# Queries of the first 128 tokens taken block by block through the weight, and the third input tile's load held behind GpSimd's constants

## The chip, the cores and the metric

The kernel runs on one core of one Trainium2 chip. The metric is device time in microseconds (us) for one execution of the whole program. Before the change the median of three runs is 266.89 us (266.51, 266.89 and 267.87).

## What is computed

One transformer block with two parallel branches on 2048 tokens of width 640. Both branches read the same layer-normed input, and the result is their sum with the residual:

```python
x = A_x
xn = _layernorm(x, axis=-1)
return x + _A_ref(xn, A_wqkv, A_wo) + _B_ref(xn, B_w_gate, B_w_up, B_w_down)
```

Branch A is attention in 32 heads of width 20. Each token looks at 8 earlier tokens, itself included, two positions apart. `q`, `k` and `v` come from one product with `wqkv` (640 x 1920), and the result goes through `wo` (640 x 640). Branch B is a gated layer without a non-linearity: `(xn @ w_gate) * (xn @ w_up)`, width 1536, then `w_down`. All tensors are bf16.

## The kernel before, in words

The 2048 tokens are 16 tiles of 128, and four tiles make a chunk of 512 (`c`, with `ttl` the tile in it). The width of 640 is five blocks of 128 (`KT` = 5). A weight such as `wq` lies in SBUF as five row blocks `wq[:, i, :]`, one for each block `i` of the contraction; its columns are five output blocks `j`.

For each tile, `norm` (L383) takes the statistics on VectorE (L390, L397, L403: `bn_stats` of two halves, then `bn_aggr` into `mv`), the reciprocal root on GpSimd (L410, `rstd`), and the normalisation on VectorE (L419, `xn_t`). The tiles of chunk 0 are turned by TensorE (L458, `pst`), and ScalarE copies the result to `xnT` (L480); for tile 0, VectorE copies blocks 3 and 4. Later chunks are turned by DMA (L440).

Then come the products: `qk_group` (L504) for q and k, each output block `j` a group of five matmuls over `i` (L514, `psqk`), evicted by ScalarE to `qkT` (L531); `v_tile` (L548) for v (L558, `psv`); `gu` (L589) for the gate and the up product (L600, `psg`, `psu`); the logits (L660 on VectorE, `pw`; L676 on TensorE, `lps`); the weighted sum over v on VectorE (L786 to L800); and the last product with the residual (L849, L856, L879). v has another order of columns, so GpSimd permutes its weight first, one row block at a time: five copies `wv[:, i, :]` from `wo` (L308). Matmul `i` of the first v group waits for copy `i`.

The loads at the start are on three queues. ScalarE's queue issues `wq` in three transfers, of row blocks 0-1, 2-3 and 4 (L284). SyncE (SP) issues x tiles 0 to 3 (L261), `wk` and the v weight, which lies in the buffer `wo` for now (L269), x tile 4, the zeroed halo (L297), then x tiles 5 onward as their buffers come free (there are five). GpSimd's queue issues `wg` and `wu` (L326) after the four `rstd` of chunk 0. Ahead of all that GpSimd writes constants: the identity, the masks and others (L172 to L195), the last of them `mb` (L192).

The order of the work on each engine isn't written out by hand. Each piece of work is a step with an engine, an assumed cost, the steps it waits for, the pool buffers that it takes and a priority. `Plan.run` (L76) plays the steps on a model of the engines and emits them in the order that comes out. What an engine then does on the chip is fixed: it takes its instructions in that order and waits at each for the semaphores that it needs. A transfer from SP or ScalarE also waits until the transfer eight places earlier in the plan's order has landed, since eight semaphores go round.

TensorE's order in the head is: ten matmuls on zeros (L371), the turn of tile 0, three more on zeros, q of tile 0 in the groups `[0, 1]`, `[2]`, `[3, 4]` with the turn of tile 1 after the first of them, q of tile 1, turn of tile 2, k of tile 0, turn of tile 3, q of tile 2, and the other q and k products; then two gate and two up groups, and v. For tile 0 this is set by:

```python
groups = ([0, 1], [2], [3, 4], [5, 6, 7], [8, 9])
```

so the first ten matmuls run over all five row blocks of `wq` for output blocks 0 and 1.

Of the kernel before, what the change touches and what calls it, by code (L numbers as in the profile page):

```python
# [9 lines left out]
ACT = mybir.ActivationFunctionType  # L10
# [20 lines left out]
class Plan:  # L31
# [9 lines left out]
    def token(self, pool):  # L41
        return Token(pool)

    def add(self, eng, cost, fn, deps=(), prio=0.0, lag=0.0, takes=(), reads=(),
            nbytes=0, tight=False):
        s = Step(eng, cost, fn, deps, prio, lag, list(takes), list(reads), nbytes,
                 tight)
        for t in s.reads:
            t.left += 1
        self.steps.setdefault(eng, []).append(s)  # L50
        return s
# [65 lines left out]
def kernel(  # L117
# [11 lines left out]
    nc = tc.nc  # L129
    P = nc.NUM_PARTITIONS  # L130
# [8 lines left out]
    HALO = DIL * (W - 1)  # L139
    scale = float(Dh) ** -0.5  # L140
    EPS = 1e-5
    KT = D // P
# [7 lines left out]
    bf16, f32 = dt.bfloat16, dt.float32  # L150
# [8 lines left out]
    psum = ctx.enter_context(  # L159
        tc.tile_pool(name="psum", bufs=NPS, space=bass.MemoryType.PSUM)  # L160
    )
# [8 lines left out]
    with tc.manual_schedule():  # L170
# [32 lines left out]
        wq = const.tile([P, KT, D], bf16, name="wq")  # L203
# [20 lines left out]
        G = {}  # L224
        add, token = plan.add, plan.token

        def tl(name, shape, dtype, bufs):
            return work.tile(shape, dtype, name=name, tag=name, bufs=bufs)


        mm512, mm320, mm256, mm128 = 0.216, 0.136, 0.11, 0.057

        def act(n):
            return 0.06 + n / 1200.0
# [11 lines left out]
        def dma(fn, nbytes, deps=(), prio=None, takes=(), reads=(), q="SP", n=1, lag=0.0):  # L246
            if prio is None:
                spn[0] += 1
                prio = -5000.0 + spn[0]
            return add(q, n * issue[q], lambda: fn(queues[q]), deps=deps, prio=prio,  # L250
                       lag=lag, takes=takes, reads=reads, nbytes=nbytes)
# [4 lines left out]
        def load_x(t, ahead=0):  # L256
            T_x[t] = token("x")

            def fn(q):
                G["x", t] = tl("x_t", [P, D], bf16, 5)  # L260
                q.dma_start(  # L261
                    out=G["x", t][:], in_=x_flat[t * P : (t + 1) * P, :]
                )

            S_x[t] = dma(fn, P * D * 2 + ahead, takes=[T_x[t]])
# [13 lines left out]


        S_wq = []
        for lo, hi in ((0, 2), (2, 4), (4, KT)):
            def ld(lo=lo, hi=hi):
                nc.scalar.dma_start(  # L284
                    out=wq[:, lo:hi, :],
                    in_=A_wqkv[lo * P : hi * P, 0:D].rearrange("(i p) f -> p i f", p=P),
                )

            S_wq.append(add("ACT", 0.45, ld, prio=-5000.0 + lo, lag=4.45))
# [91 lines left out]
        S_xnT, T_xnT, S_tr, S_rs, S_xn = {}, {}, {}, {}, {}  # L381
# [115 lines left out]
        S_qk, T_qk, S_v, S_vst = {}, {}, {}, {}  # L497

        def qk_tile(c):
            if ("qk", c) not in G:  # L500
                G["qk", c] = tl("qkT", [P, 2 * KT, HALO + CS], bf16, 2)
            return G["qk", c]

        def qk_group(c, js, cols, prio):  # L504
            n = cols.stop - cols.start
            T = token("ps")

            def mm():
                ps = psum.tile([P, 512], f32, name="psqk", tag="ps")
                for a, j in enumerate(js):  # L510
                    w = wq if j < KT else wk
                    jj = j % KT
                    for i in range(KT):
                        nc.tensor.matmul(  # L514
                            ps[:, a * n : (a + 1) * n],
                            lhsT=w[:, i, jj * P : (jj + 1) * P],
                            rhs=G["xnT", c][:, i, cols],
                            start=(i == 0), stop=(i == KT - 1),
                        )
                G["psqk", c, js[0], cols.start] = ps  # L520

            tts = range(cols.start // P, cols.stop // P)
            deps = [d for q in tts for d in S_xnT[c, q]]
            deps += S_wq if min(js) < KT else []
            deps += [S_wk] if max(js) >= KT else []
            m = add("PE", len(js) * KT * (0.003 + n / 2400.0), mm, deps, prio, lag=0.15,
                    takes=[T], reads=[T_xnT[c]], tight=c == 0)

            def ev():
                ps = G["psqk", c, js[0], cols.start]  # L530
                nc.scalar.copy(  # L531
                    qk_tile(c)[:, js[0] : js[-1] + 1,
                               HALO + cols.start : HALO + cols.stop],
                    ps[:, 0 : len(js) * n].rearrange("p (j s) -> p j s", j=len(js)),
                )

            takes = []
            deps = [m]
            if c not in T_qk:
                T_qk[c] = token("qk")  # L540
                takes = [T_qk[c]]
                S_qk[c] = []
            else:
                deps.append(S_qk[c][0])
            S_qk[c].append(add("ACT", act(len(js) * n), ev, deps, prio, lag=0.1,
                               takes=takes, reads=[T]))

        def v_tile(c, ttl, prio):  # L548
            t = c * CH + ttl
            T_vt = token("vt")  # L550
            evs = []
            for n in range(2):
                T = token("ps")

                def mm(n=n):
                    ps = psum.tile([P, 512], f32, name="psv", tag="ps")
                    for i in range(KT):
                        nc.tensor.matmul(  # L558
                            ps[:, 0:HS],
                            lhsT=G["xnT", c][:, i, ttl * P : (ttl + 1) * P],  # L560
                            rhs=wv[:, i, n * HS : (n + 1) * HS],
                            start=(i == 0), stop=(i == KT - 1),
                        )
                    G["psv", t, n] = ps

                m = add("PE", KT * mm320, mm, S_xnT[c, ttl] + S_wv, prio, lag=0.15,
                        takes=[T], reads=[T_xnT[c]])

                def ev(n=n):
                    if n == 0:  # L570
                        G["vt", t] = tl("v_t", [P, D], bf16, 3)
                    nc.scalar.copy(  # L572
                        G["vt", t][:, n * HS : (n + 1) * HS], G["psv", t, n][:, 0:HS]
                    )

                evs.append(add("ACT", act(HS), ev, [m] + evs, prio, lag=0.1,
                               takes=[T_vt] if n == 0 else [], reads=[T]))

            def st(q):
                q.dma_start(  # L580
                    out=vD[HALO + t * P : HALO + (t + 1) * P, :], in_=G["vt", t][:]
                )

            S_vst[t] = dma(st, P * D * 2, evs, prio, reads=[T_vt], q="POOL")
# [317 lines left out]
        load_gu(0, 0.4, [S_wk, S_rs[CH - 1]])  # L902
        for ttl in range(CH):
            cols = slice(ttl * P, (ttl + 1) * P)
            groups = ([0, 1], [2], [3, 4], [5, 6, 7], [8, 9])
            if ttl:
                groups = ([0, 1], [2, 3, 4], [5, 6, 7], [8, 9])
            for a, js in enumerate(groups):
                qk_group(0, js, cols, 10.0 + ttl + 0.1 * a + (2.05 if js[0] >= KT else 0.0))
        for ttl in range(CH):  # L910
            v_tile(0, ttl, 14.0 + ttl)
# [1 line left out]
        def qkv(c, prio):  # L913
            for ttl in range(CH):
                norm(c, ttl, -2000.0 + 10 * c + ttl)
            for j in range(2 * KT):
                qk_group(c, [j], slice(0, CS), prio + 0.1 * j)
            for ttl in range(CH):
                v_tile(c, ttl, prio + 2 + ttl)
# [61 lines left out]
```

## Time and profile before

| | before |
|---|---|
| median of three runs | 266.89 us |
| the profiled execution | 268.14 us |
| its span, first to last instruction | 266.4 us |
| around the span | 1.74 us |
| TensorE busy | 260.7 us, 98% |
| VectorE busy | 209.1 us, 78% |
| ScalarE busy | 105.7 us, 40% |
| GpSimd busy | 38.5 us, 14% |
| mean granted TensorE clock | 0.994 |
| HBM read and written | 35.39 and 5.26 MB |

Times within the execution are counted from the start of the span. A line of the timeline has the start, the length, the engine, the line of the kernel, the operation, output and inputs, and in brackets the idle time ahead of it with what ended it. A line of the chain has start, length, engine or DMA, and work. A line of the windows has, for a stretch of time, its length and then for PE (TensorE), PEld (its weight loads), DVE (VectorE), ACT (ScalarE) and POOL (GpSimd) the busy time and the number of instructions, then the granted clock (PEclk, 1.00 is full), the busy share of the DMA engines, and GB/s. Matmuls are pipelined, and the chain gives each the time that it adds, so the two views differ by some 0.2 us at a matmul's start.

### The profile page before, as it was taken

The page shows a single profiled execution, that of the slowest core. Times are in us where ns is not written, and L with a number is a line of the kernel's source. Part 1 is how long each engine was busy: PE and PEld are TensorE (multiplying, and loading weights), DVE is VectorE, ACT ScalarE, POOL GpSimd, SP SyncE. Part 2 cuts the span into 40 slices and gives each one's busy share as a digit, 9 for nine tenths or more (in the row PEclk, how much of TensorE's full clock was granted, in tenths as well). Part 3 has the DMA queues.
Part 4 walks back from the last instruction along what each step waited for, and adds up shares of the span by engine and source line. Part 5 has one row for each costly group of instructions (what it writes and reads, how often), then busy time and mean ns, then how long its engine had stood idle before and what let it go on. Part 6 is the DMA issues. An engine that isn't in the chain of part 4 may idle for free.

```text
span 266.4 us, 4439 instructions
## 1 busy us (share of the span) xinstructions
PE 260.7 (98%) x1744; PEld 149.4 (56%) x1744; DVE 209.1 (78%) x284; ACT 105.7 (40%) x193; POOL 38.5 (14%) x62
## 2 busy tenths in 40 slices
PE   7899999999999999999999999999999999999995
PEld 2796644544456744754466654644446664445775
DVE  5498978999999805999999429999986479998221
ACT  2365555565542236135520165155550105555000
POOL 5578860250001100000000000100000000000000
PEclk9799999999999999999999999999999999999999
DMA  7996699769799990169785620598931301782211
GB/s 219 362 349 107 174 380 240 248 195 260 222 225 272 252 263 0 50 173 286 225 258 117 160 60 0 155 272 250 248 86 46 94 25 32 217 234 64 74 49 49
DMA packets 52016, 46.57 MB, mean 175 GB/s; under 512 B 25038, under 2 KB 50076, under 8 KB 51996
## 3 DMA queue, kind: packets, MB, share of 16 engines
q1 hardware_dynamic: 48780, 36.09, 50.9%
q0 software_dynamic: 2384, 9.34, 10.6%
q10 hardware_dynamic: 832, 0.87, 1.0%
q8 instruction: 13, 0.21, 0.3%
q14 instruction: 7, 0.06, 0.1%
HBM read 35.39 MB, written 5.26 MB: 153 GB/s over the span
## 4 chain that ended last, share of the span: by engine, by line
PE 96%; DMA 2%; ACT 0%; DVE 0%; issue 0%
PE psd L856 20%; PE psu L600 19%; PE psg L600 19%; PE psqk L514 17%; PE psd L849 8%; PE psv L558 8%; PE lps L676 4%; DMA wq<-in_A_wqkv_dram 2%; PE pst L458 0%; ACT L200 0%; DVE ob L879 0%
## 5 line engine op out<-in xcount | busy, mean ns | idle before, releaser
L600 PE MATMUL psu<-xnT,wu 128*128 128x512 bf16 x240 | 59.5, 379 | 0.0
L600 PE MATMUL psg<-xnT,wg 128*128 128x512 bf16 x240 | 59.2, 379 | 0.0
L856 PE MATMUL psd<-wd,hT 128*128 128x320 bf16 (+2 forms) x396 | 57.7, 295 | 0.0
L660 DVE TENSOR_TENSOR pw<-qkT 128x2560 bf16<-128x2560 bf16 x32 | 46.4, 1483 | 4.9 <-PE lps L676 2.9
L856 PEld LDWEIGHTS <-hT 128*128 128x128 bf16 x396 | 38.1, 98 | 14.1
L786 DVE TENSOR_TENSOR v<-v,a 128x5120 bf16<-128x5120 bf16 x16 | 45.1, 2819 | 0.3 <-DMA v<-vD 0.2
L615 ACT CAST gs<-psg 128x512 bf16<-128x512 f32 x48 | 28.1, 586 | 32.6 <-PE psg L600 32.1
L615 ACT CAST us<-psu 128x512 bf16<-128x512 f32 x48 | 28.1, 585 | 32.4 <-PE psu L600 32.3
L600 PEld LDWEIGHTS <-wu 128*128 128x128 bf16 x240 | 23.4, 98 | 28.2 <-issue 0.4
L600 PEld LDWEIGHTS <-wg 128*128 128x128 bf16 x240 | 23.3, 98 | 27.8 <-issue 0.4
L879 DVE TENSOR_TENSOR ob<-psd,xr 128x320 bf16<-128x320 f32 (+2 forms) x33 | 15.6, 476 | 25.4 <-PE psd L856 25.2
L531 ACT CAST qkT<-psqk 128x512 bf16<-128x512 f32 (+3 forms) x47 | 24.3, 522 | 19.7 <-PE psqk L514 19.1
L849 PE MATMUL psd<-wo,oT 128*128 128x320 bf16 (+2 forms) x165 | 27.1, 295 | 0.0
L514 PE MATMUL psqk<-xnT,wq 128*128 128x128 bf16 (+1 forms) x175 | 24.3, 302 | 1.4 <-DMA wq<-in_A_wqkv_dram 1.3
L797 DVE TENSOR_TENSOR v<-v 128x2560 bf16<-128x2560 bf16 x16 | 23.8, 1484 | 0.0
L558 PE MATMUL psv<-wv,xnT 128*128 128x320 bf16 x160 | 23.2, 299 | 0.0
L514 PE MATMUL psqk<-xnT,wk 128*128 128x128 bf16 (+1 forms) x175 | 22.8, 288 | 0.0
L580 POOL DMA_DIRECT2D vD<-v_t x16 | 8.9, 555 | 94.7 <-ACT v_t L572 93.6
L572 ACT CAST v_t<-psv 128x320 bf16<-128x320 f32 x32 | 13.5, 427 | 21.5 <-PE psv L558 18.0
L514 PEld LDWEIGHTS <-wq 128*128 128x128 bf16 x175 | 14.3, 105 | 10.6 <-DMA wq<-in_A_wqkv_dram 1.4
L849 PEld LDWEIGHTS <-oT 128*128 128x128 bf16 x165 | 15.8, 98 | 7.5 <-issue 0.8
L558 PEld LDWEIGHTS <-xnT 128*128 128x128 bf16 x160 | 15.5, 98 | 7.4 <-issue 0.8
(55 smaller groups left out, 169.8 us busy)
## 6 DMA issues: line engine op xcount, KB each, us to landing
v<-vD SPq DMA_DIRECT2D x16, 1280.0 KB, 6.3
x_t<-in_A_x_dram SPq DMA_DIRECT2D x16, 160.0 KB, 4.1
vD<-v_t POOLq DMA_DIRECT2D x16, 160.0 KB, 3.4
out_dram<-ob SPq DMA_DIRECT2D x15, 160.0 KB, 2.6
wg<-in_B_w_gate_dram POOLq DMA_DIRECT2D x2, 960.0 KB, 8.0
wu<-in_B_w_up_dram POOLq DMA_DIRECT2D x2, 960.0 KB, 10.9
wd<-in_B_w_down_dram POOLq DMA_DIRECT2D x1, 1920.0 KB, 9.5
xr<-in_A_x_dram SPq DMA_DIRECT2D x12, 160.0 KB, 4.2
```

What stands on the lines that cost most here:

```text
L514: nc.tensor.matmul(ps[:, a * n : (a + 1) * n], lhsT=w[:, i, jj * P : (jj + 1) * P], rhs=G["xnT", c][:, i, cols], start=(i == 0), stop=(i = ...
L531: nc.scalar.copy(qk_tile(c)[:, js[0] : js[-1] + 1, HALO + cols.start : HALO + cols.stop], ps[:, 0 : len(js) * n].rearrange("p (j s) -> p j ...
L558: nc.tensor.matmul(ps[:, 0:HS], lhsT=G["xnT", c][:, i, ttl * P : (ttl + 1) * P], rhs=wv[:, i, n * HS : (n + 1) * HS], start=(i == 0), stop ...
L572: nc.scalar.copy(G["vt", t][:, n * HS : (n + 1) * HS], G["psv", t, n][:, 0:HS])
L600: nc.tensor.matmul(ps[:], lhsT=wt[h][:, i, ff * P : (ff + 1) * P], rhs=G["xnT", c][:, i, :], start=(i == 0), stop=(i == KT - 1),)
L615: nc.scalar.copy(g[:], G["ps" + nm, c, f][:])
L660: nc.vector.tensor_tensor(pt[:], qk[:, 0:KT, HALO:], qk[:, KT:, o : o + CS], ALU.mult)
L786: nc.vector.tensor_tensor(v, v, G["a16", c][:, ttl, :, None, :].to_broadcast([P, W, Dh, H]), ALU.mult,)
L797: nc.vector.tensor_tensor(v8[:, 0:4], v8[:, 0:4], v8[:, 4:8], ALU.add)
L849: nc.tensor.matmul(G["psd", t, n][:, 0:wide], lhsT=G["oT", t][:, g, :], rhs=wo[:, g, cols], start=(g == 0), stop=False,)
L856: nc.tensor.matmul(G["psd", t, n][:, 0:wide], lhsT=G["hT", c, f][:, ttl * P : (ttl + 1) * P], rhs=wd[:, f, cols], start=False, stop=(f == ...
L879: nc.vector.tensor_tensor(G["ob", t][:, cols], G["psd", t, n][:, 0:wide], G["xr", t][:, cols], ALU.add,)
```

## The change

Two things are changed.

First, q of tile 0 no longer goes through `qk_group` but through `first_q`. It computes the five output blocks in two PSUM banks (blocks 0, 1, 2 and blocks 3, 4), and its outer loop is over the three row ranges of `wq`, as they are transferred: ten matmuls of row blocks 0-1, ten of 2-3, five of 4. Each of the three steps waits for its own transfer alone. Two evictions on ScalarE follow the last step. The number and the shapes of matmuls are unchanged.

Second, when x tile 2 is loaded, GpSimd first writes a zero into the tile's first column, and the transfer overwrites it. So the transfer waits for GpSimd, which comes to this write after the last of its constants. SP's queue is in order, so what stands behind waits too.

The order of instructions on TensorE, by shape, and on VectorE is the same as before. ScalarE copies the turned tile 1 ahead of the evictions of tile 0's q, where one of the latter came first. Because x tile 2 now comes after `wq` in the plan's order, the semaphores that go round are dealt out otherwise: the issue of x tile 5 waits for `wq`'s second transfer where it waited for x tile 3, that of x tile 6 for `wq`'s third where it waited for `wk`, that of x tile 7 for x tile 2, and that of x tile 8 for x tile 3.

```diff
             def fn(q):
                 G["x", t] = tl("x_t", [P, D], bf16, 5)
+                if t == 2:
+
+                    nc.gpsimd.memset(G["x", t][:, 0:1], 0.0)
                 q.dma_start(
...
-        for lo, hi in ((0, 2), (2, 4), (4, KT)):
+        Q_ROWS = ((0, 2), (2, 4), (4, KT))
+        for lo, hi in Q_ROWS:
...
+        def first_q(prio):
+            banks = ([0, 1, 2], [3, 4])
+            T = [token("ps") for _ in banks]
+            m = None
+            for b, (lo, hi) in enumerate(Q_ROWS):
+                def mm(lo=lo, hi=hi):
+                    for a, js in enumerate(banks):
+                        if lo == 0:
+                            G["psqk", 0, js[0], 0] = psum.tile(
+                                [P, 512], f32, name="psqk", tag="ps"
+                            )
+                        ps = G["psqk", 0, js[0], 0]
+                        for n, j in enumerate(js):
+                            for i in range(lo, hi):
+                                nc.tensor.matmul(
+                                    ps[:, n * P : (n + 1) * P],
+                                    lhsT=wq[:, i, j * P : (j + 1) * P],
+                                    rhs=G["xnT", 0][:, i, 0:P],
+                                    start=(n == 0 and i == 0), stop=(i == KT - 1),
+                                    skip_group_check=True,
+                                )
+
+                m = add("PE", KT * (hi - lo) * mm128, mm,
+                        (S_xnT[0, 0] if hi > 3 else S_xnT[0, 0][:1]) + [S_wq[b], m],
+                        prio + 0.01 * b, lag=0.15, takes=[] if lo else T,
+                        reads=[T_xnT[0]], tight=True)
...
-            groups = ([0, 1], [2], [3, 4], [5, 6, 7], [8, 9])
-            if ttl:
-                groups = ([0, 1], [2, 3, 4], [5, 6, 7], [8, 9])
-            for a, js in enumerate(groups):
+            groups = ([0, 1], [2, 3, 4], [5, 6, 7], [8, 9])
+            if ttl == 0:
+                first_q(10.0)
+                groups = groups[2:]
+            for a, js in enumerate(groups, 4 - len(groups)):
```

More of the change, by code (lines that the diff above doesn't have):

```diff
@@ L546, in qk_group, with ev @@
                                takes=takes, reads=[T]))
+        def first_q(prio):
[23 more added lines that the diff above has]
+                        reads=[T_xnT[0]], tight=True)
+            T_qk[0] = token("qk")
+            S_qk[0] = []
+            for n, js in enumerate(banks):
+                def ev(js=js):
+                    nc.scalar.copy(
+                        qk_tile(0)[:, js[0] : js[-1] + 1, HALO : HALO + P],
+                        G["psqk", 0, js[0], 0][:, 0 : len(js) * P].rearrange(
+                            "p (j s) -> p j s", j=len(js)
+                        ),
+                    )
+                S_qk[0].append(
+                    add("ACT", act(len(js) * P), ev, [m] + S_qk[0], prio + 0.01 * n,
+                        lag=0.1, takes=[] if n else [T_qk[0]], reads=[T[n]])
+                )
         def v_tile(c, ttl, prio):
```

## The prediction, made before the changed kernel ran

> **What bounds the kernel now.** I read the engine table first: TensorE is busy for 260.7 of 266.4 us. TensorE's waits show three only, all ahead of 8 us: 1.3 us for the zeros, 0.3 us for `xn_t`, 1.3 us for `wq`. So what the change can win lies in the head, and it counts only if no other wait takes it back. The chain of the first 30 us, in order of time, shows the work that sets the end:
>
> ```profile
> 1.78 6.16 DMA wq<-in_A_wqkv_dram
> ...
> 7.98 1.07 PE psqk L514 x8
> 9.05 0.53 PE pst L458 x5
> 9.58 3.16 PE psqk L514 x40
> 12.74 0.28 PE pst L458 x5
> 13.02 1.40 PE psqk L514 x25
> 14.42 0.28 PE pst L458 x5
> 14.70 6.98 PE psqk L514 x125
> 21.68 2.16 PE psg L600 x10
> 23.83 2.16 PE psu L600 x10
> ```
>
> A second transfer of `wq` runs until 7.94 us, then TensorE goes on without a gap. At 13.02, 25 matmuls take 1.40 us, 56 ns each; at 9.58, 40 take 3.16 us, 79 ns each. The windows say why:
>
> ```profile
> 4.57:7.98 3.41, 1.73 (x13) 0.78 (x12) 2.87 (x10) 0.48 (x1) 0.98 (x2) 1.00 1.03 349
> 7.98:11.40 3.42, 3.42 (x32) 3.30 (x33) 1.76 (x7) 1.41 (x4) 2.61 (x4) 0.50 1.06 370
> 11.40:14.81 3.41, 3.41 (x63) 3.41 (x62) 1.66 (x5) 2.47 (x7) 2.05 (x3) 1.00 1.05 369
> ```
>
> The granted clock is 0.50 from 7.98 to 11.40, after 3.41 us in which TensorE was busy for 1.73 us. The wait for `wq` thus costs 1.3 us of standing still and 1.7 us (half of 3.42) of slow work.
>
> The other chain in the head isn't TensorE's. GpSimd permutes the weight of v, in five copies with the `rstd` of tiles 4 to 8 between them:
>
> ```profile
> 20.53 1.31 POOL L308 COPY wv<-wo 128x640 bf16<-128x640 bf16 x1
> 21.80 0.55 POOL L410 TENSOR_TENSOR rstd<-mv,half_t 128x1 f32<-128x1 f32 x1
> 22.30 2.49 POOL L308 COPY wv<-wo 128x640 bf16<-128x640 bf16 x1
> ```
>
> ```profile
> 20.17 0.49 DVE L390 BATCH_NORM_STATS2 st<-x_t 128x6 f32<-128x320 bf16 x1 [0.29 <-DMA x_t<-in_A_x_dram]
> ...
> 21.09 0.24 DVE L403 BATCH_NORM_AGGREGATE mv<-st 128x2 f32<-128x18 f32 x1
> 22.12 1.49 DVE L660 TENSOR_TENSOR pw<-qkT 128x2560 bf16<-128x2560 bf16 x1 [0.79 <-ACT qkT L531]
> ```
>
> The fifth copy ends at 24.79 us. TensorE's fifth v matmul, the first that needs it, starts at 26.37: 25.83 for the first plus 4 times 0.136 (6.11 us for 45). So v's weight is only 1.58 us ahead.
>
> **The change part by part.** *q of tile 0.* 25 matmuls before and after; what moves is what they wait for. Before, the third waits for row blocks 2-3. Now ten need only row blocks 0-1, whose transfer lands at 5.2 (issue 1.31, to landing 3.9). From 6.45, where q starts now, 10 x 56 ns ends at 7.01. The turn of tile 1 has its `xn_t` by 6.74 (6.29 + 0.45) and takes 0.28: 7.29. The next fifteen need the other two transfers, which the second part sets.
>
> *x tile 2's wait.* The added write is a GpSimd memset of 0.10 us (row of `half_t`); constants end at 3.40 (2.95 + 0.45) and GpSimd idles until 4.43, which hides it. SP issues tile 2 at about 3.55 instead of 1.7 (third of four issues of 0.45 from 0.81). Behind it stand tile 3, `wk`, the v weight, tile 4, each 0.4 to 0.5 apart: 4.0, 4.4, 4.85, 5.3 instead of 2.2, 2.68, 3.15, 3.84. `wq` meanwhile shares the DMA engines with less. Its landings now (7.94, and 2.29 + 5.9 = 8.2) bound them from above; from below, 819 KB plus tiles 0 and 1 (328 KB) at 358 GB/s, the rate between 3.4 and 4.2 when tiles 0 and 1 were through, is 3.2 us from 2.0: 5.2. I take 7.3 and 7.9, the times at which TensorE wants them, because at the shared rate of 270 to 350 GB/s 1.15 MB takes 3.3 to 4.2 us, ending at 5.3 to 6.2, and landings came 0.4 to 1.7 later.
>
> Is `wk` later? It landed at 10.4 (2.68 + 7.7), and the x tiles and weights ahead of it, 2.29 MB, kept the DMA at 0.9 to 1.06 busy from 2 us on. The same bytes stand ahead of it now, so I take 10.4. Bounds: -0.23 (the rate of 253 GB/s between 4.2 and 5.0 rises to 358) and +1.7 (it follows its issue). Tile 4 and the v weight, 13.12 and 12.65, have the same bounds, with +1.4 for tile 4's issue; I take -0.1, nearest to full DMA.
>
> *ScalarE.* Tile 1's copy (0.69) goes first, from 7.4 to 8.05; the evictions, 0.48 and 0.37 instead of 0.37, 0.27 and 0.37, follow and hold nobody (ScalarE is busy 15 of the first 30 us).
>
> *Semaphores dealt otherwise.* SP waited 2.3 us for `wk` at tile 6's issue; that goes, and tiles 6 to 8 are issued earlier. Tile 8's statistics waited 0.29 us for it; that may go, hidden below.
>
> *TensorE's new path.* 7.29, fifteen matmuls 0.84: 8.13. q of tile 1, 25 x 56 ns: 9.53. Turn of tile 2: 9.81. Wait for `wk`: 10.4. k, 1.40; turn, 0.28; 125 matmuls, 6.98: 19.06. Gate and up, 4.32 (wg landed at 9.83 + 7.3 = 17.1, wu at 10.87 + 9.9 = 20.8; TensorE wants them at 19.06 and 21.2): 23.4. Four v matmuls: 23.9. Before, that point is 26.37 by starts. The lead is 2.5 us.
>
> *What is late next* is the fifth copy. Its chain starts with tile 4's landing, 13.12. VectorE's first `pw` waited 0.79 us for ScalarE's last `qkT`; that is early now, so `pw` comes right after `mv`, at 21.35, into the fourth copy (20.53 to 21.84). Where the two meet, one stands until the other is done: the fifth copy took 2.49 instead of 1.31 and ended 1.18 after `pw`; `xn_t` at 16.30 took 1.15 beside a copy. So `pw` runs 21.84 to 23.24 (1.40), the `rstd` ends 0.42 behind it (as at 32.99, 1.41 us, beside a `pw` to 33.98), and the last copy takes 23.61 to 24.92. If the `rstd` goes first, 22.35 + 1.43 + 1.18 = 24.96, the same. GpSimd to VectorE took 0.05, so the fifth matmul starts at 24.97, and with tile 4's -0.1 at 24.87 instead of 26.37.
>
> *Sum:* -1.5 us. The profiled execution would take 268.14 - 1.5 = 266.6, span 264.9; it is 1.25 above the median, from which I count: 266.89 - 1.5 = 265.4. Behind the head it should stay won: VectorE waits for TensorE again at 39.80 (1.90 us for `lps`) and for ScalarE at 45.33 (1.23), so its saturated stretch starts earlier with TensorE; the turned outputs land at 75.2 and 82.1, 1.9 and 2.0 us ahead of use.
>
> **The rivals.** *The copies don't bind:* only if tile 4 lands over 1 us early; against it, the DMA is full. The lead of 2.5 then counts: 264.4.
>
> *No slow clock in the timed runs:* the three differ by 1.36 us, about what the slow stretch is worth: where the clock stays at 1.00, TensorE comes 1.7 us earlier and already stands at the fifth copy (24.79 against 24.67), so little is left, 0.1 to 0.2: 266.7. Whether it falls depends on where the 3.41 us lie against the wait. The Trainium skill, "TensorE: Matmul & The Clock Gate", Part 1, says these windows run freely and don't start with the kernel; one trace can't show that.
>
> *The new pause slows the clock:* TensorE stands for 1.0 us from 23.9 and 0.6 us ahead of `wk`. 1.73 us busy in 3.41 was little enough for 0.50; here it is 2.4 or more, so I think not. If it does, 1.7: 267.1. The same part of the skill warns of pauses above some 3.4 us; by that rule this rival couldn't be, nor the slow stretch before, whose pause was 1.3 us. There the measurement decides.
>
> *Slower: tile 4 follows its issue.* If it lands 1.4 us late while `wk` comes on time, the fifth copy ends at 26.3, TensorE gains nothing, and stands for 2.5 us from 23.9. Then a window holds 0.9 us of work, less than the 1.73, and the slow clock costs 1.7: 268.6. It decides from a delay of about 1 us. For it: the issue is 1.4 us later. Against: tile 4's 9.3 us to landing was queueing.
>
> **How the numbers follow.** Forecast 0.56 (its own range 265.0 to 266.2, for tile 4 from -0.4 to +0.7); copies not binding 0.07; no slow clock before 0.17; clock slowed anew 0.07; slower 0.13. A measurement here tells about 0.5% from no change, 1.33 us, so faster means below 265.56: two thirds of the forecast and the first rival, 0.37 + 0.07 = 0.44. Within 0.5%: 0.19 + 0.17 + 0.07 = 0.43. Slower: 0.13. The range, 264.4 to 267.2, leaves out the slower case and some edges.
>
> **What would show it.** Right: no wait for `wq`, PEclk 1.00 at 8 us, k of tile 0 at 10.4 behind a wait for `wk`, a wait for GpSimd's `wv` copy at about 24, v's fifth matmul at 24.9. Wrong: `st` waits for tile 4 beyond 13.4; the copies end after 25.5; a window of 0.50 after 11 us; a new wait on `lps` or `oT`.

## The result and the profile after

The changed kernel takes 267.78 us (median of 22 runs, 266.1 to 269.11). The kernel before, run beside it on the same chip, takes 266.8 us (22 runs). The ratio is 1.0032, 95% interval 1.0017 to 1.0046. So the change makes the kernel 1.0 us slower by the medians, where 1.5 us faster was forecast; 267.78 also lies above the range of 264.4 to 267.2. The profiled execution of the changed kernel takes 268.06 us with a span of 266.4 us and a mean granted clock of 1.00.

The chain of the first 32 us, after, in order of time (start, length, work):

```profile
3.40 0.06 POOL x_t L263
...
3.47 0.33 SPq L264
...
4.32 7.37 DMA wk<-in_A_wqkv_dram
...
11.73 1.57 PE psqk L518 x25
...
23.09 1.80 POOL rstd L414
24.89 1.27 POOL wv L312
...
26.20 5.73 PE psv L606 x41
```

Read it from the top: the added write ends GpSimd's constants, SP then issues x tiles 2 and 3 and, at 4.32, `wk`. Its transfer lands at 11.69, not at 10.4, and TensorE waits. In the end the chain runs through GpSimd's copies, and the fifth v matmul starts at 26.20. TensorE's waits over the whole execution, after (total, times, longest), name the same two places and no `wq` any more:

```profile
PE psqk L518 <- DMA wk<-in_A_wqkv_dram: 1.5, 1, 1.5
PE wps L375 <- DVE zt L197: 1.3, 1, 1.3
PE psv L606 <- POOL wv L312: 0.8, 1, 0.8
```

The window from 7.98 us, which showed a clock of 0.50 before, is at 1.00 now, and so is the one ahead of it (the columns are those of before):

```profile
4.57:7.98 3.41, 3.28 (x36) 2.17 (x35) 2.82 (x9) 0.79 (x2) 1.08 (x2) 1.00 1.00 342
7.98:11.40 3.42, 2.27 (x39) 2.03 (x36) 1.84 (x7) 2.59 (x6) 2.54 (x4) 1.00 1.05 362
```

The timeline of VectorE and GpSimd shows the statistics of x tile 4 and the first copy. In brackets is how long each stood, and for which transfer:

```profile
14.41 0.49 DVE L394 BATCH_NORM_STATS2 st<-x_t 128x6 f32<-128x320 bf16 x1 [3.97 <-DMA x_t<-in_A_x_dram]
...
14.00 1.32 POOL L312 COPY wv<-wo 128x640 bf16<-128x640 bf16 x1 [2.17 <-DMA wo<-in_A_wqkv_dram]
```

Tile 4 came at 13.12 before and comes at 14.41 now, the v weight at 12.65 and now at 13.9. So what stands behind tile 2 on SP's queue is 1.3 us late, and the end of the head follows it. Two of the signs that the prediction named as proof against it are there: `st` waits beyond 13.4, and the copies end after 25.5 (at 26.15).

### The profile page after: what moved, and what is told of

Its sections match the earlier page's. It is cut to its first block, busy times and chain, and to the rows that moved or that the text cites. A ratio compares the mean times of both kernels' runs of the same rounds, so it can differ in the third digit from the quotient of the medians.

```text
span 266.4 us, 4422 instructions
## 1 busy us (share of the span) xinstructions
PE 259.0 (97%) x1727; PEld 148.0 (56%) x1744; DVE 209.9 (79%) x284; ACT 104.7 (39%) x192; POOL 38.1 (14%) x63
## 4 chain that ended last, share of the span: by engine, by line
PE 91%; DMA 3%; POOL 2%; DVE 1%; issue 1%; SPq 0%; POOLq 0%
PE psd L904 20%; PE psu L648 19%; PE psg L648 18%; PE psqk L518 15%; PE psd L897 8%; PE psv L606 8%; PE lps L724 4%; DMA wk<-in_A_wqkv_dram 3%; POOL rstd L414 1%; POOL wv L312 1%; DVE xn_t L423 1%; SPq L264 0%; POOL mb L192 0%; DVE st L401 0%; DVE mv L407 0%
## 5 line engine op out<-in xcount | busy, mean ns | idle before, releaser
L648 PE MATMUL psg<-xnT,wg 128*128 128x512 bf16 x230 | 58.6, 379 | 0.5
L708 DVE TENSOR_TENSOR pw<-qkT 128x2560 bf16<-128x2560 bf16 x32 | 47.2, 1508 | 3.9 <-ACT qkT L535 2.5
L904 PEld LDWEIGHTS <-hT 128*128 128x128 bf16 x396 | 38.0, 98 | 14.3 <-DVE hT L672 0.2
L663 ACT CAST us<-psu 128x512 bf16<-128x512 f32 x48 | 28.1, 586 | 30.6 <-PE psu L648 29.4
L535 ACT CAST qkT<-psqk 128x512 bf16<-128x512 f32 (+2 forms) x44 | 23.2, 536 | 16.8 <-PE psqk L518 16.3
L518 PE MATMUL psqk<-xnT,wq 128*128 128x128 bf16 (+1 forms) x147 | 21.0, 297 | 0.2
L672 DVE TENSOR_TENSOR hT<-gs,us 128x512 bf16<-128x512 bf16 x48 | 18.8, 416 | 0.5 <-ACT us L663 0.5
```

The lines of the kernel that those rows point to most:

```text
L518: nc.tensor.matmul(ps[:, a * n : (a + 1) * n], lhsT=w[:, i, jj * P : (jj + 1) * P], rhs=G["xnT", c][:, i, cols], start=(i == 0), stop=(i = ...
L535: nc.scalar.copy(qk_tile(c)[:, js[0] : js[-1] + 1, HALO + cols.start : HALO + cols.stop], ps[:, 0 : len(js) * n].rearrange("p (j s) -> p j ...
L648: nc.tensor.matmul(ps[:], lhsT=wt[h][:, i, ff * P : (ff + 1) * P], rhs=G["xnT", c][:, i, :], start=(i == 0), stop=(i == KT - 1),)
L663: nc.scalar.copy(g[:], G["ps" + nm, c, f][:])
L672: nc.vector.tensor_tensor(hT[:], G["gs", c, f][:], G["us", c, f][:], ALU.mult)
L708: nc.vector.tensor_tensor(pt[:], qk[:, 0:KT, HALO:], qk[:, KT:, o : o + CS], ALU.mult)
```

## The experiments

Three questions: which half of the change costs the time (theory L: the wait, because it makes the transfers land late; rival Q: q by row blocks), why q by row blocks brings nothing (theory C: the slow clock of the profiled execution before isn't typical), and, later, where an earlier head is lost. The compared `before` is always run on the same chip beside them.

**before_again**: the kernel before, once more, with no edit.

> The kernel before, unchanged, to see its clock in more executions. Theory C: its profiled execution, 268.14 against a median of 266.8, was one with the slow clock (mean 0.994); most executions show 1.00 and take 266.5 or so, with v's fifth matmul at about 24.9, held by the fifth copy. Rival: all executions show 0.994, and the profile is typical.

Measured: 266.89 us, ratio 0.9992 (0.9973 to 1.0012). In all ten executions the mean clock is 0.999 or 1.00. In the profiled one (span 264.7) TensorE waits 0.7 us for `wq` where it waited 1.3, and the windows have no 0.50 (TensorE is busy 2.56 of the 3.41 us ahead, where it was 1.73):

```profile
4.57:7.98 3.41, 2.56 (x19) 1.18 (x18) 2.97 (x10) 0.48 (x1) 1.07 (x2) 1.00 1.05 370
7.98:11.40 3.42, 3.42 (x64) 3.35 (x61) 1.78 (x7) 2.35 (x7) 2.60 (x4) 1.00 1.07 365
```

v starts at 23.97 and runs through without a wait for GpSimd:

```profile
23.97 3.83 PE L558 MATMUL psv<-wv,xnT 128*128 128x320 bf16 x27
```

Its fifth matmul is 4 x 0.136 later, at 24.51, against 26.37 in the execution that the prediction was worked out from. Of 124 executions of `before` run beside the experiments, 9 have a mean clock of 0.994 (268.07 to 268.93 us each), which is the mean of the execution with one slow window (half of 3.42 in 266.4 us); the others are at 0.999 or above. Theory C holds: the 1.7 us of slow work that the change was to remove is there in at most some 7 of 100 executions. For those nine there is no trace, so where in them the slow stretch lies isn't shown.

**wait_alone**: the kernel before with the second part alone.

```diff
                 G["x", t] = tl("x_t", [P, D], bf16, 5)
+                if t == 2:
+                    nc.gpsimd.memset(G["x", t][:, 0:1], 0.0)
```

> The kernel before with only the write that holds x tile 2 back. Theory L: wk lands at 11.7 and tile 4 at 14.4, as in the changed kernel; the fifth copy ends at 26.1, and the time is the changed kernel's, 267.6 to 268.0 (+1.0 us). Rival Q: no loss, 266.5 to 267.0.

Measured: 267.97 us, ratio 1.005 (1.0034 to 1.0067). `wk` lands at 11.55, the v weight at 13.8, tile 4 at 14.3, and the fifth v matmul starts at 26.06.

**q_alone**: the changed kernel without the two lines above.

> The changed kernel without the write that holds x tile 2 back; q of tile 0 still goes by row blocks. Theory L (late landings): the wait alone costs, by making wk and tile 4 land 1.3 us later (11.7 and 14.4 instead of 10.4 and 13.1), so that v's fifth matmul stands until 26.2 for the fifth permuting copy. Then here wk lands at 10.4, tile 4 at 13.1, the fifth copy ends at 24.8 to 25.0, and the time is 1.0 to 1.4 us below the changed kernel: about 266.5, level with before or up to 0.4 us better. Rival Q (the block-wise q costs by itself, through its banks, its evictions or the order on ScalarE): the time stays at 267.5 to 268.

Measured: 266.59 us, ratio 1.0003 (0.9982 to 1.0024). `wk` lands at 10.5, and the fifth v matmul starts at 24.98. So the wait alone makes the whole loss and q by row blocks alone is neutral: L, not Q. This rests on the medians of ten and twelve executions. The profiled execution of q_alone is the slowest of its twelve, 268.89 us, though its head is on time: what comes behind the head differs between executions by as much as the head does.

**short_wait** and **mid_wait**: the changed kernel, with the added write moved ahead in GpSimd's order. In short_wait the masks `Ek` and `mb` come behind it, so that x tile 2 is issued at 1.7 as before; in mid_wait only `mb` does, and the issue is at about 2.7. The edit of mid_wait:

```diff
         mb = const.tile([P, W, H], bf16, name="mb")
-        nc.gpsimd.memset(mb[:], 0.0)
...
+        def make_mb():
+            nc.gpsimd.memset(mb[:], 0.0)
...
                     nc.gpsimd.memset(G["x", t][:, 0:1], 0.0)
+                    make_mb()
```

> The changed kernel with the write put ahead of the constants Ek and mb, so that x tile 2 is issued at about 1.7 us, as before the change, while the order of transfers and of the semaphores stays that of the changed kernel. Theory L with the delay as its cause: wk at 10.4, tile 4 at 13.1, time about 266.5. Rival O (not the delay but the order dealt out anew, or one DMA engine that lags for another reason): landings at 11.7 and 14.4 and a time of 267.6 to 268.0.

> The changed kernel with the write put ahead of the constant mb alone, so that x tile 2 is issued at about 2.7 us, between 1.7 (no loss) and 3.5 (loss of about 1.0 us). If the landings follow the issue in proportion: wk at 11.0, tile 4 at 13.7, the last permuting copy ends at 25.5, and the time is 267.2 to 267.4. If the delay costs only beyond a point: wk at 10.5, tile 4 at 13.2, and 266.6 to 266.9, or all of the loss, 267.7 to 268.0.

Measured: short_wait 266.91 us, ratio 1.0008 (0.999 to 1.0027), `wk` at 10.5 and the fifth v matmul at 25.02. mid_wait 267.06 us, ratio 1.0002 (0.998 to 1.0025); `wk`, issued at 3.56, lands at 9.5, as early as in any execution with no delay, and v runs from 23.35 without a wait. So the write, its semaphore and the other deal of semaphores cost nothing that these intervals show. In the head the loss isn't in proportion to the delay: none at 1.0 us, and 1.3 us at 1.8 in the profiled execution of the changed kernel. The times alone don't show that, since the interval of mid_wait reaches to 0.7 us of loss, and the head of mid_wait is one execution.

**wk_on_act**: the changed kernel with `wk` issued on ScalarE's queue, not behind x tile 2.

```diff
-        S_wk = load_qkv(1, wk)
+        S_wk = dma(
+            lambda e: nc.scalar.dma_start(
+                out=wk[:],
+                in_=A_wqkv[:, D : 2 * D].rearrange("(i p) f -> p i f", p=P),
+            ),
+            2 * P * KT * D,
+        )
```

> The changed kernel with wk issued on ScalarE's queue, behind wq at about 2.8 us, while x tiles 2 and 3, the v weight and tile 4 stay on SP behind the wait. If landings are late because the issue is late: wk at 10.5 or earlier, but the v weight and tile 4 still at 13.5 to 14.4, so TensorE comes to v at 23.5 and stands for the last copy until 26: 267.5 to 267.9. If what counts is the bytes that go ahead: tile 4 at 13.1 again and 266.5 to 266.8.

Measured: 269.19 us, ratio 1.0082 (1.0052 to 1.0112), slower than either expectation. `wk` is issued at 2.81 and takes 8.3 us: 11.1, late in spite of its early issue. x tile 2, issued at about 3.5 on the other queue, isn't there until 11.3, and TensorE stands 3.6 us for it. So a late landing isn't simply a late issue. The 160 KB of x tile 2 took 7.8 us beside the 800 KB of `wk`; in the changed kernel, where `wk` stands behind it on the same queue, they took 3.4.

**swap** and **q_swap**: the changed kernel and q_alone, with x tile 4 issued ahead of the v weight, since the copies' chain starts with tile 4.

```diff
-        for t in range(CH, 2 * CH):
+        load_x(CH)
+        S_wr.fn, S_x[CH].fn = S_x[CH].fn, S_wr.fn
+        for t in range(CH + 1, 2 * CH):
```

> The changed kernel, wait included, with the transfers of x tile 4 and of the v weight issued in the opposite order; the order on the compute engines is the same. wk still lands at 11.7, so TensorE comes to v at 24.7 as in the changed kernel. Theory L, that tile 4's late landing holds the permuting copies and these hold TensorE: tile 4 lands at 12.2, the v weight at 14.3, the last copy ends by 25, v's fifth matmul starts at 25.3 instead of 26.2, and the time falls by 0.5 to 0.9 us, to 266.9 to 267.3. Rival, that the wait for wk is the loss and the copies are not: 267.6 to 268.0.

> q by row blocks, no wait on x tile 2, and tile 4 ahead of the v weight. Theory L: wk at 10.5, tile 4 at 11.0, the v weight at 13.1; the copies end at 22.2 to 23.6, ahead of TensorE's fifth v matmul at 24.1, which was at 24.98 with the block-wise q alone. If nothing takes the 0.9 us back the time is 265.7 to 266.1. Rival: VectorE's work on the logits and the turned outputs, which ran late in one profile of the block-wise q, takes it back: 266.4 to 266.8.

Measured: swap 267.49 us, ratio 1.0008 (0.998 to 1.0037); q_swap 266.79 us, ratio 0.9995 (0.9973 to 1.0016). The head does what it should: tile 4 lands at 11.76 in swap, whose fifth v matmul starts at 25.33, and in q_swap v runs from 23.73 without a wait. The total doesn't follow: swap stays above the 266.9 to 267.3 expected, and q_swap is level with before. With q_swap 0.24 us, and mid_wait 0.62 us, ahead of before_again at v's first matmul, the profiled executions of both end behind it (spans 265.9 and 266.6 against 264.7). These two are slower than the medians of their kernels (267.6 against 266.79, 268.27 against 267.06), and that of before_again is the fastest of its ten, so by the medians the lead brings nothing rather than a loss.

Where the lead goes in these executions is seen at 40 us. The timeline of ScalarE and that of VectorE in q_swap, then its windows from 32 us:

```profile
44.54 0.43 ACT L619 CAST v_t<-psv 128x320 bf16<-128x320 f32 x1 [2.81 <-DMA vD<-v_t]
```

```profile
45.49 2.90 DVE L707 TENSOR_TENSOR pw<-qkT 128x2560 bf16<-128x2560 bf16 x2 [3.41 <-ACT qkT L534]
```

```profile
32.00:36.00 4.00, 4.00 (x21) 1.77 (x19) 3.97 (x7) 2.24 (x4) 3.73 (x4) 1.00 1.02 348
36.00:40.00 4.00, 4.00 (x34) 1.60 (x33) 3.55 (x4) 1.87 (x4) 1.34 (x3) 1.00 1.04 380
40.00:44.00 4.00, 4.00 (x33) 2.08 (x34) 2.08 (x2) 1.17 (x2) 0.00 (x0) 1.00 1.01 248
```

ScalarE has three `v_t` buffers. For the fifth tile of v it needs the buffer of the second, whose store goes out at 33.8, behind the second half of the gate and up weights (two loads of 960 KB, issued from 30.6) on GpSimd's queue. All DMA engines are busy, the store lands at 44.5, and ScalarE, in order, can't evict the last `qkT` until then. VectorE stands 3.4 us for that `qkT`. In before_again the same lines are:

```profile
43.31 0.43 ACT L572 CAST v_t<-psv 128x320 bf16<-128x320 f32 x1 [1.44 <-DMA vD<-v_t]
```

```profile
44.26 4.30 DVE L660 TENSOR_TENSOR pw<-qkT 128x2560 bf16<-128x2560 bf16 x3 [2.03 <-ACT qkT L531]
```

The store goes out no earlier in q_swap than there (33.80 and 33.70), though v starts earlier, and it takes 10.7 us until `v_t` goes on, against 9.6. In mid_wait these are 33.51 and 10.4 us. So in these executions the store, and not the head, decides when this `pw` starts; why it takes up to 1.1 us longer isn't shown.

**before_late**, **q_swap_late**, **after_late**: before, q_swap and the changed kernel, with the second half of those weights issued behind the stores of the first chunk. TensorE first reads them near 58 us. The planner also moves work later in the kernel.

```diff
             S_mark = add("POOL", 0.1, seen(("xnT", 1), KT - 1, slice(CS - 1, CS)),
-                         S_xnT[1, CH - 1], 0.9, reads=[T_xnT[1]])
+                         S_xnT[1, CH - 1] + [S_vst[CH - 1]], 0.9, reads=[T_xnT[1]])
```

> Before with one edit: the second half of the gate and up weights (wg, wu; 960 KB each) is issued on GpSimd's queue behind the stores of the first chunk's four v tiles, not between the first and the others; these weights are first read near 60 us. The planner also moves later work. In the runs so far those 1.9 MB go out at 30.5 to 33.4, all 16 DMA engines are busy to about 43, the store of v tile 1 takes 9.5 us from issue to landing, and ScalarE, which has three v_t buffers, stands 1.4 to 2.8 us before its next v_t and holds up qkT and with it VectorE's pw of the second chunk. Theory D (this stall sets the start of the second chunk's pw): the store lands in some 4 us, ScalarE's wait for the store falls under 0.7 us, pw of the second chunk starts 1 to 2 us earlier than the 44.3 of before, and the time falls to 265.0-266.3. Rival E (VectorE is full from 45 to 90 whatever starts it, or the weights are late in their turn): 266.6-268.5.

> The kernel with q by row blocks and tile 4 ahead of the v weight, no wait on GpSimd (266.79), with the same edit as before_late. Theory D, which says that the full DMA engines took back the earlier head: ScalarE's wait of 2.8 us for the store falls under 0.7 us and the kernel comes out 0.2-0.7 us under before_late. If the lead of the head is lost in another place, it equals before_late within 0.2 us.

> The changed kernel with the same edit as before_late. If the wait of the third x tile costs in the head alone and nothing downstream absorbs it, it stays 0.9-1.3 us over before_late. If the full DMA engines at 30 to 43 us were part of the loss, the distance falls under 0.5 us.

Measured: before_late 266.28 us, ratio 0.9972 (0.9951 to 0.9992); q_swap_late 265.88 us, ratio 0.996 (0.9937 to 0.9982); after_late 266.99 us, ratio 0.9992 (0.9968 to 1.0015). In q_swap_late VectorE's line is:

```profile
42.38 1.49 DVE L707 TENSOR_TENSOR pw<-qkT 128x2560 bf16<-128x2560 bf16 x1 [0.76 <-ACT qkT L534]
```

It is 3.1 us earlier than in q_swap, though only 0.4 of that lies in the start of v (23.36). The lead of q_swap_late over before_late is 0.9 us at the start of v (24.28 there), 0.9 at this `pw` (43.30), 1.0 in the span (263.9 against 264.9) and 0.4 in the medians. So in the profiled executions what the head wins is kept where the stores no longer stand behind the weights, as theory D says. The medians agree, but 0.4 us between twelve executions each isn't clear of their spread (265.65 to 267.08, and 266.01 to 266.65). The theory was off in a detail: ScalarE's waits for the store sum to 1.1 to 1.5 us, not under 0.7, but now lie near 30 us, as one `v_t` is planned earlier, and none is left ahead of this `pw`. after_late stays 0.7 us over before_late, between the two expectations. That before_late gains some 0.75 us by itself may in part be the planner's other moves, which weren't separated. q_swap_late is the fastest version found: its interval lies below 1, so it is faster than before, and it is 1.1 us below after_late, run beside it.

One thing didn't fit: the head of after_late is that of the changed kernel, with the same issue times, but `wk` landed at 10.5 and the fifth v matmul started at 25.01.

**after_a**, **after_b**, **after_c**, **wait_b**: the changed kernel three times more and wait_alone once more, on one chip, with no edit.

> The changed kernel again, unchanged. So far with the third x tile issued at 3.5 us and wk at 4.3, wk landed at 11.7 (after), 11.55 (wait_alone) and 11.3 (swap), but at 10.5 in after_late, whose head is the same. Theory V (the late landing belongs to the single execution: one or two DMA engines lag in most of them): the three repeats differ, some landing near 10.5 with the fifth v matmul at 25.0 and a total near 266.1-266.9, others near 11.6 with 26.1 and 267.4-268.2. Theory F (it is fixed by the kernel, and after_late's head was another chip's): all three land within 0.2 us of each other.

> As after_a: a second execution of the changed kernel to look at, on the same chip. Theory V: its landing of wk differs from the first one's by over 0.2 us in at least one of the pairs. Theory F: none does.

> As after_a: a third execution of the changed kernel to look at, on the same chip. Theory V: its landing of wk differs from the first one's by over 0.2 us in at least one of the pairs. Theory F: none does.

> The wait alone (before and the memset, q unchanged) again. By theory V its wk lands near 10.5 or near 11.6 as it happens; by theory F it lands with the other three of this call.

Measured: 268.26, 267.61, 267.93 and 268.19 us; ratios 1.0028 (0.9991 to 1.0065), 1.0019 (0.9982 to 1.0056), 1.0036 (0.999 to 1.0083) and 1.0028 (0.9993 to 1.0063) (the intervals don't tell them from each other or from before). What counts here are the profiled executions, which took 268.28, 267.02, 268.94 and 268.78 us. TensorE in after_a, then in after_b, the same program:

```profile
11.86 1.57 PE L518 MATMUL psqk<-xnT,wk 128*128 128x128 bf16 x25 [1.37 <-DMA wk<-in_A_wqkv_dram]
...
26.34 3.83 PE L606 MATMUL psv<-wv,xnT 128*128 128x320 bf16 x27 [0.80 <-POOL wv L312]
```

```profile
10.48 1.56 PE L518 MATMUL psqk<-xnT,wk 128*128 128x128 bf16 x25
...
24.42 5.73 PE L606 MATMUL psv<-wv,xnT 128*128 128x320 bf16 x41 [0.27 <-POOL wv L312]
```

after_c is like after_a (11.64 and 26.07), wait_b too (12.00 and 26.43). Theory V holds in that the landing belongs to the single execution. All profiled executions with `wk` behind x tile 2, by the issue of x tile 2:

| x tile 2 issued at | `wk` landed at | in |
|---|---|---|
| 1.7 us | 9.6 to 10.5 | before, before_again, before_late, q_alone, short_wait, q_swap, q_swap_late |
| 2.7 us | 9.5 | mid_wait |
| 3.5 us | 9.9, 10.5 | after_b, after_late |
| 3.5 us | 11.3 to 12.0 | after, after_a, after_c, wait_alone, wait_b, swap |

The trace shows what is late. For each transfer it has sixteen semaphore events, one for the share of each of the 16 DMA engines, and the transfer has landed with the last of them. For `wk` in after_b all sixteen come from 9.08 to 9.88 us. In after fourteen come by 9.53, the fifteenth at 10.26 and the last at 11.69. The theory's "one or two DMA engines" isn't general, though: in after_a three come after 11 us (11.02 to 11.81), in swap six (11.02 to 11.29), and in after_c seven (10.84 to 11.60). The DMA engines as a whole are less full in these executions too. The windows from 6 to 9 us in after_b, then in after_c:

```profile
6.00:9.00 3.00, 3.00 (x42) 2.75 (x41) 2.37 (x8) 1.39 (x3) 1.10 (x2) 1.00 1.06 363
```

```profile
6.00:9.00 3.00, 2.87 (x47) 2.61 (x45) 2.77 (x8) 1.84 (x4) 0.93 (x2) 1.00 0.83 250
```

In the six late executions these three microseconds have 249 to 338 GB/s, in all others of the table 347 to 374. In after it is 323, where before had 360; a faster start made up for it, so that both had moved 2.28 MB by 9 us. A sign comes earlier still: SP's issue of tile 4, at 5.4 us, took 0.53 us in after_b and after_late, and 0.93 to 1.11 in the five late executions with the same order. The Trainium skill, "DMA: Bandwidth & Descriptors", section "Why a DMA increments its semaphore by 16 and not by 1", says that the engines of one transfer finish independently and that the semaphore counts all of them; the trace agrees, with 2.2 us between the fourteenth event and the sixteenth in after.

## Why the prediction was wrong

*q of tile 0 by row blocks.* Right: q starts at 6.64 (6.45 predicted), no wait for `wq` is left, and TensorE is ready for k at 10.2 (9.8 predicted).

*The clock.* Right for the changed kernel: 1.00 throughout the profiled execution, also beside the new pause of 1.5 us. Of its 22 timed executions one has a mean clock of 0.994 (269.11 us).

*"The same bytes stand ahead of it now, so I take 10.4", and tile 4 "-0.1, nearest to full DMA".* This is the step that failed first. The bytes are indeed the same, and in after_b and after_late `wk` landed by the time forecast, or earlier. But in six of eight profiled executions with this issue time it lands 0.9 to 1.6 us later, and the profiled one has tile 4 at +1.3, near the upper bound of +1.4. The DMA engines weren't as full as assumed (323 GB/s from 6 to 9 us, where before had 360), and a full average says nothing of the last of sixteen. That the wait makes the loss of 1.0 us is shown by wait_alone, q_alone and short_wait, and the traces show the late `wk` and tile 4 with it. Why engines lag with an issue at 3.5 us, and not in seven executions with 1.7 and one with 2.7, stays open.

*The chain of the fifth copy.* Right in mechanism: 24.97 was predicted for a tile 4 at 13.12; after_late, with tile 4 at 13.21, has 25.01, q_alone 24.98, short_wait 25.02. With tile 4 at 14.41 the same chain gives 26.26; the changed kernel has 26.20.

*"It is 1.25 above the median, from which I count."* This failed too. The lead of 1.5 us was measured against an execution with the slow clock and then taken off a median of executions without it. Against before_again's 24.51 the forecast 24.87 is no lead at all. It is the larger part of the miss: short_wait, the changed kernel with its loads on time and the fifth v matmul at 25.02, gains nothing (ratio 1.0008), where 1.5 us were forecast; the late landing then adds its 1.0 us. That is the rival "no slow clock in the timed runs", which had 0.17 and should have had most. The rival named one sign, the 1.36 us between the three runs; the 1.25 us between the profiled execution and the median were a second. The Trainium skill, "TensorE: Matmul & The Clock Gate", Part 1, has free-running windows; that nine executions in 124 of one program have a lower mean clock agrees with this.

*"Behind the head it should stay won."* Failed for the kernels as they stand: in the profiled executions ScalarE's wait for the store of `v_t` takes the lead back (q_swap, mid_wait, and after_b, where that wait is 2.7 us and VectorE's `pw` starts at 45.43, 1.2 us after before_again's). The prediction had looked at what VectorE waits for at 45.33, not at what that eviction waited for.

*The slower rival.* Its mechanism came, in another form. It let tile 4 follow its issue with `wk` on time, one pause of 2.5 us and a slow clock: 268.6. Both were late, so TensorE's pause fell into 1.5 and 0.8 us, the clock stayed at 1.00, and the loss was 1.0 us. The range ended at 267.2 because this case was left out of it.

*The sum.* The head of the changed kernel is 26.20 - 24.51 = 1.7 us behind before_again, and the two profiled executions differ by 268.06 - 266.45 = 1.6. That these two agree is in part luck, since before_again's execution is 0.4 below its own median. The medians differ by 1.0, and two of the eight profiled executions with this issue time had `wk` on time; how many of the timed ones did isn't on record.

## What to carry to other kernels

Before a gain is worked out from one profiled execution, put its time beside the median: if the difference is about what the stall or the slow clock in it is worth, the stall may be in that execution alone. A load that is held back need not cost anything (mid_wait), but its landing is that of its last DMA engine, so look at several executions before taking full DMA as a reason that a later issue is free. And follow a lead to the next full resource: here a store behind 1.9 MB of weights that nobody needed for 20 us took it back. The edit that puts the weights behind the stores brought 0.75 us, with whatever else the planner moved. q by row blocks brought nothing by itself; together with tile 4 ahead of the v weight, and with the stores out of the way, it was 0.4 us better by the medians, and which of the two does that wasn't separated.

## What the hardware showed that was not expected

The landing of one transfer of 800 KB, with the same program and issue time, differs between four executions of the changed kernel by 1.9 us (9.9 to 11.8). In the three later ones one, three and seven of its sixteen shares came after 10.5 us, and from 6 to 9 us the DMA engines moved 363 GB/s in the earliest of the four and 250 to 323 in the others. A transfer of 160 KB took 7.8 us beside one of 800 KB that had been issued 0.7 us earlier on another queue and took 8.3 (wk_on_act); with the 800 KB behind it on its own queue it took 3.4.
